# Delta rule and feed-forward on one core: the first stretch of the feed-forward written out in joint bursts

## Chip, core and metric

The kernel runs on one core of a Trainium2 chip. A core has five engines with a queue each: TensorE (PE, matmuls and transposes, with its weight loads shown apart), VectorE (DVE), ScalarE (ACT), GpSimd (POOL) and SyncE (SP), which here issues nearly all transfers. Each engine works its own instructions in the order of the program and waits where an operand isn't ready. The metric is the device time of one execution in microseconds (us). Before the change it is 678.54 us, the median of 4 runs (677.17 to 681.86).

## What is computed

A delta-rule attention over 4 sequences of 768 tokens with 8 heads of 48 dimensions, and behind it a feed-forward block with a PReLU, 384 to 2048 to 384, all in float32:

```python
k_n = k / (np.linalg.norm(k, axis=-1, keepdims=True) + 1e-06)
for t in range(S):
    kt, vt, bt = (k_n[:, :, t], v[:, :, t], beta[:, :, t, None])
    y[:, :, t] = np.einsum('bhd,bhde->bhe', q[:, :, t], state)
    v_old = np.einsum('bhde,bhd->bhe', state, kt)
    state = state + bt[:, :, :, None] * np.einsum('bhd,bhe->bhde', kt, vt - v_old)
x = y.transpose(0, 2, 1, 3).reshape(B * S, H * D)
h = x @ w_in
g = np.maximum(h, 0.0) + alpha * np.minimum(h, 0.0)
return g @ w_out
```

## The kernel before, in words

**Chunks and steps.** The 768 tokens are cut into 12 chunks of 64. Within a chunk the recurrence is written as a triangular system, so that it becomes matmuls. A step is one chunk of one pair of sequences; there are 24, and steps 2c and 2c + 1 make chunk c. Steps 0 and 1 are done ahead of everything in `first_chunk`. The stretch that the change touches holds steps 2 and 3, together with the feed-forward's first layer for chunk 0.

**What a step needs.** `flips` transposes keys and queries (128x128 transposes, line 360) and ACT copies them out (381, 383). `squares` and `weigh` make the norms and weights: ACT 330, 340, 341, DVE 332, 347, POOL 349, 350. `grams` multiplies keys with keys (407) and DVE weights the result into `same` and `right` (413); POOL copies a part on (456). Four steps together are turned (`turn_in`, DVE 472) and eliminated on DVE. For the first four steps only 16x16 blocks are eliminated; `cross` puts the 32x32 inverses together from them with 32x32 products: 576, an ACT copy (581), 586 and 593, then DVE adds (600, 602). `placing` lays the inverses into `diag` and `inv` (ACT 631) and copies weights (652). `between_1` (663) and `between_2` (677) make the 64x64 inverse, with an ACT copy (669) and a DVE addition (684) behind them. `through_state` multiplies with the state (713, 718) and DVE subtracts and masks (728, 427), ACT copies `y` (736). `solve` is 743 with DVE 747, `outputs` 756 with 762, `next_state` 772 with 780. `to_ffn` transposes `y` (795) into `xt` (ACT 797).

**The feed-forward's first layer.** `ffn_in(0)` issues 48 products of 128 rows by 256 columns (884), in eight groups of six. Each group has one of two PSUM banks; ACT 894 and DVE 896 empty it. `IN_PARTS` is 48.

**The weights.** `w_in` and `w_out` come from memory as float32 words that are converted in pieces. A piece is a pair of ACT instructions (208, 209) and a pair of DVE instructions (218, 223), and a fetch by SP (192) where a staging place comes free. `conv_in` and `conv_out` are the generators of these; the touched stretch has 22 halves of pieces.

**What sets the order.** The queues are written by hand: every engine executes what the program emits, in that order. `weave` takes several generators and a number of parts for each, and draws from them in turn in proportion. `part(g, n)` draws n parts; `chain` puts generators behind each other.

**Around the change.** Before it, `first_chunk` ends with the transposes of steps 0 and 1. In the stretch itself one `weave` draws from four sources: the products of `ffn_in(0)`; the attention of steps 2 and 3 (`in_turn(*later)`, `ready(2)`, `pair(2)`); the weight pieces; and `statics(4, 7)`, the transposes and Grams of steps 4 to 7. Within `cross` a callback (`aside`) puts one product of `ffn_in(0)` between every four or eight blocks. Behind the stretch comes a `weave` of the remaining `w_out` pieces, `ffn_in(1)`, more `statics`, and the elimination of steps 4 to 7.

Small tiles in PSUM come from `ps_big`, which has three buffers of two banks in rotation: a new one has to wait until the one three allocations earlier has been emptied.

## Time and profile before

| what | before |
|---|---|
| median of 4 runs | 678.54 us |
| profiled execution | 680.26 us |
| its span | 678.5 us |
| PE busy | 657.1 us (97%) |
| DVE busy | 453.3 us (67%) |
| ACT busy | 263.7 us (39%) |
| POOL busy | 35.5 us (5%) |
| PE busy, 50.5 to 97.0 us | 45.58 of 46.50 us |
| DVE busy, same stretch | 31.88 us |
| ACT busy, same stretch | 29.77 us |
| mean busy share of the DMA engines, same stretch | 0.73 |
| granted TensorE clock, same stretch | 1.00 |

The busy time of PE is a time in which a matmul was under way, and not a measure of how well it was used: matmuls are pipelined, and a row's duration contains its way through the array. What a matmul costs the stream is therefore read from the starts of consecutive rows. The idle time in brackets on a timeline's row is what the engine waited before it, with the instruction that released it.

### The profile page before, as it was taken

The numbers are of one execution on the slowest core, as the hardware profiler recorded it, in microseconds if no ns is written. First come the engines' busy times: TensorE is split into PE (matmuls) and PEld (weight loads), VectorE is DVE, ScalarE is ACT, GpSimd is POOL, SyncE is SP. The second block draws the span as 40 slices with busy tenths as digits, with TensorE's granted clock in tenths as the row PEclk, the third lists the DMA queues.
The fourth block names the chain that finished last, engine by engine and source line by source line (L and its number), as shares of the span: only waits on it lengthen the run. The fifth ranks groups of instructions, "written<-read, shape, count | busy, mean of one in ns | idle before, by whom it ended". The sixth has DMA issues, their size and how long they took to land.

```text
span 678.5 us, 21573 instructions
## 1 busy us (share of the span) xinstructions
PE 657.1 (97%) x9359; PEld 572.6 (84%) x9359; DVE 453.3 (67%) x1125; ACT 263.7 (39%) x624; POOL 35.5 (5%) x105
## 2 busy tenths in 40 slices
PE   5999998999998999999999999999999999999997
PEld 4577777656687998988998988988989989989997
DVE  4955788878989868758858758859655355354251
ACT  5926756335455343344353342243234134021110
POOL 6000211101000000001000000000000000000000
PEclk9979999999999999999999999999999999999999
DMA  8937854211332022122111112111121110100000
GB/s 123 242 90 203 201 116 117 71 30 30 71 76 49 12 62 48 25 48 49 26 37 37 26 37 37 26 40 33 26 46 27 36 37 2 33 5 2 23 1 25
DMA packets 110960, 37.69 MB, mean 56 GB/s; under 512 B 104161, under 2 KB 107249, under 8 KB 110865
## 3 DMA queue, kind: packets, MB, share of 16 engines
q1 hardware_dynamic: 109088, 35.81, 24.2%
q8 instruction: 74, 1.21, 0.7%
q10 hardware_dynamic: 1776, 0.49, 0.4%
q14 instruction: 22, 0.17, 0.1%
HBM read 31.56 MB, written 4.72 MB: 53 GB/s over the span
## 4 chain that ended last, share of the span: by engine, by line
PE 81%; DVE 11%; ACT 4%; SPq 2%; issue 1%; DMA 0%; POOL 0%; DVEq 0%
PE p_ffn L884 33%; PE p_ffn L948 27%; PE p_big L360 2%; PE p_big L713 2%; PE p_big L743 2%; PE p_big L756 2%; PE p_big L663 2%; DVE prod L499 2%; PE p_big L677 2%; DVE block L505 2%; PE p_big L1104 2%; SPq L120 1%; PE p_big L718 1%; PE p_big L407 1%; PE p_big L772 1%
## 5 line engine op out<-in xcount | busy, mean ns | idle before, releaser
L884 PE MATMUL p_ffn<-xt,w_in 128*128 128x256 f32 x1152 | 265.2, 383 | 5.1 <-DVE act L896 2.3
L884 PEld LDWEIGHTS p_ffn<-xt,w_in 128*128 128x128 f32 x1152 | 213.3, 190 | 35.1 <-ACT sums L894 2.2
L896 DVE SCALAR_TENSOR_TENSOR act<-act,al_t,p_ffn 128x256 f32<-128x256 f32 x176 | 76.5, 476 | 82.1 <-ACT act L894 82.1
L894 ACT ACTIVATE act<-p_ffn 128x512 f32<-128x512 f32 x88 | 52.4, 596 | 146.6 <-PE p_ffn L884 146.2
L948 PE MATMUL p_ffn<-w_out,act 128*128 128x192 f32 x480 | 82.5, 328 | 0.1
L948 PEld LDWEIGHTS p_ffn<-w_out,act 128*128 128x128 f32 x480 | 77.6, 190 | 1.1 <-issue 0.5
L505 DVE TENSOR_TENSOR block<-block,prod 128x30 f32<-128x30 f32 (+9 forms) x150 | 49.9, 333 | 5.1
L499 DVE TENSOR_TENSOR prod<-block 128x30 f32<-128x30 f32 (+9 forms) x150 | 48.8, 325 | 3.3 <-POOL block L489 1.6
L968 DVE TENSOR_TENSOR o_sb<-u,p_ffn 128x192 f32<-128x192 f32 x40 | 13.4, 353 | 52.2 <-PE p_ffn L948 41.9
L797 ACT COPY xt<-p_big 128x384 f32<-128x384 f32 x22 | 10.4, 477 | 75.7 <-PE p_big L795 75.7
L736 ACT COPY y<-p_big 128x384 f32<-128x384 f32 x22 | 10.5, 477 | 51.4 <-PE p_big L718 49.9
L948 PE MATMUL p_ffn<-space_out,sums 128*128 128x192 f32 x160 | 29.4, 327 | 0.0
L948 PE MATMUL p_ffn<-more,sums 128*128 128x192 f32 x160 | 29.3, 326 | 0.0
L948 PE MATMUL p_ffn<-w_out,sums 128*128 128x192 f32 x160 | 27.6, 326 | 0.0
L948 PEld LDWEIGHTS p_ffn<-more,sums 128*128 128x128 f32 x160 | 26.5, 190 | 0.0
L948 PEld LDWEIGHTS p_ffn<-space_out,sums 128*128 128x128 f32 x160 | 26.5, 190 | 0.1
L948 PEld LDWEIGHTS p_ffn<-w_out,sums 128*128 128x128 f32 x160 | 26.3, 190 | 0.0
L689 ACT COPY inv<-p_big 32x256 f32<-32x256 f32 x38 | 13.8, 362 | 29.4 <-DVE u L747 29.2
L631 ACT ACTIVATE diag<-inverse,which 64x128 f32<-64x128 f32 (+2 forms) x60 | 24.2, 405 | 2.1 <-DVE inverse L472 1.3
L728 DVE TENSOR_TENSOR r<-v_raw,p_big 64x192 f32<-64x192 f32 (+1 forms) x66 | 23.2, 352 | 1.0
L349 POOL TENSOR_TENSOR beta_t<-beta_t,rec 128x8 f32<-128x8 f32 x24 | 6.6, 274 | 304.3 <-DVE rec L347 283.7
L713 PE MATMUL p_big<-beside,k_t 48*64 48x112 f32 x704 | 21.4, 259 | 0.6 <-DVE right L413 0.6
(156 smaller groups left out, 950.7 us busy)
## 6 DMA issues: line engine op xcount, KB each, us to landing
w_out<-in_moe_w_in_dram SPq DMA_DIRECT2D x12, 512.0 KB, 4.9
qp<-in_q_dram SPq DMA_DIRECT2D x48, 96.0 KB, 3.0
v_raw<-in_v_dram SPq DMA_DIRECT2D x48, 96.0 KB, 2.9
kl<-in_k_dram SPq DMA_DIRECT2D x96, 48.0 KB, 2.6
out_dram<-o_sb SPq DMA_DIRECT2D x92, 48.0 KB, 1.6
space_out<-in_moe_w_out_dram SPq DMA_DIRECT2D x11, 384.0 KB, 3.7
ke<-in_k_dram SPq DMA_DIRECT2D x43, 96.0 KB, 3.3
w_out<-in_moe_w_out_dram SPq DMA_DIRECT2D x5, 384.0 KB, 4.0
```

What stands on the lines that cost most here:

```text
L360: nc.tensor.transpose(p[0:ROWS, g * 128 : (g + 1) * 128], src[:, 2 * g : 2 * g + 2].rearrange("p h d -> p (h d)")[:, 0:ROWS], ident,)
L499: nc.vector.tensor_tensor(out=prod, in0=r[:, 0:j, j : j + 1].to_broadcast([128, j, n]), in1=r[:, j : j + 1, j + 1 : HB].to_broadcast([128, ...
L505: nc.vector.tensor_tensor(out=r[:, 0:j, j + 1 : HB], in0=r[:, 0:j, j + 1 : HB], in1=prod, op=ALU.add)
L631: nc.scalar.mul(out, x, which[rows, i : i + 1])
L663: nc.tensor.matmul(p[half(t ^ a if changes(n) else t), a, g], right[n % EARLY][half(t), a * G + g : a * G + g + 2].rearrange("p b i -> p ( ...
L689: nc.scalar.copy(to[rows], p[rows])
L713: nc.tensor.matmul(p[half(t ^ a), a, g], k_t[n][dims(a), g, half(t)], beside[bp][dims(a), t, g])
L728: nc.vector.tensor_tensor(out=r[to, a], in0=v_in[to, a], in1=p[own, a, :, 0:D], op=ALU.subtract)
L884: nc.tensor.matmul(p_h[:, i], w_in[:, t, (f + i) * 128 : (f + i + 1) * 128], xt[:, t], start=(t == 0), stop=(t == KT - 1),)
L894: nc.scalar.activation(g, p_h, ACT.Relu, scale=-1.0)
L896: nc.vector.scalar_tensor_tensor(out=g[:, i], in0=g[:, i], scalar=al_t[:, f + i : f + i + 1], in1=p_h[:, i], op0=ALU.mult, op1=ALU.add,)
L948: nc.tensor.matmul(p, x(i), w(i), start=(i == 0), stop=(i == FP - 1))
```

## The change

The `weave` of the stretch is replaced by a function that writes the order out. At its head the 32x32 products of steps 2 and 3 come in three bursts: the 576 of both steps, then 586 and 593 of step 2, then those of step 3. Behind them are five joint bursts, in which steps 2 and 3 do the same operation one after the other, three of them followed by the Gram of one of the steps 4 to 6; the Gram of step 7 comes last. Between the bursts stand 4 to 6 products of `ffn_in(0)`, with 1 to 3 weight pieces and, once, the six placements woven into them by `alongside`. The transposes of steps 4 to 7 follow directly on a burst. `through_state` and `solve` of both steps now share one PSUM buffer for their small results, and `outputs` and `next_state` of a step share one. The functions `pair`, `ready` and `in_turn` and two constants go. The loads are issued from within the new function.

```diff
-    PAIR = 6
-    def pair(n):
...
-    READY = 5
-    def ready(n):
...
-    def in_turn(*gens):
...
-    n = PARTS_IN - n + 10
+    assert n + 22 == PARTS_IN + 10
 
     first_in = ffn_in(0)
-    later = [
-        cross(0, slice(x * H, x * H + H), edge, half_way, lambda: next(first_in, None))
-        for x in (2, 3)
-    ]
-    weave(
-        (first_in, IN_PARTS - 10), (chain(in_turn(*later), ready(2), pair(2)), 2 * CROSS + READY + PAIR),
-        (chain(conv_in, part(conv_out, 10)), n), (statics(NJ, 2 * NJ - 1), 2 * NJ + 1),
-    )
+    convert_on = chain(conv_in, part(conv_out, 10))
+
+    def alongside(products, pieces, *gens):
+        weave((part(first_in, products), products), (part(convert_on, pieces), pieces), *gens)
+
+    def second_pair():
+
+        n = 2
+        both, x = (n, n + 1), NJ
+        halves = [cross(0, slice(i * H, i * H + H), edge, half_way) for i in both]
+        squares(x)
+        alongside(4, 2)
+        for h in halves:
+            next(h)
+        flips(x, n)
+        load_early(x + NKE)
+        load_q(n + 2)
+        squares(x + 1)
+        alongside(5, 2)
+        next(halves[0])
+        flips(x + 1, n + 1)
+        load_early(x + 1 + NKE)
+        load_q(n + 3)
+        now(weigh(x))
+        place(n, (0,))
+        alongside(4, 2)
+        next(halves[1])
+        now(weigh(x + 1))
+        place(n + 1, (0,))
+        alongside(4, 2)
+        for i in both:
+            now(between_1(i))
+        now(grams(x))
+        squares(x + 2)
+        alongside(5, 3, (chain(*(placing(i, (1, 2, 3)) for i in both)), 6))
+        for i in both:
+            now(between_2(i))
+        now(grams(x + 1))
+        for i in both:
+            scale_v(i)
+        flips(x + 2, N)
+        load_early(x + 2 + NKE)
+        now(weigh(x + 2))
+        alongside(5, 3)
+        y = ps_big()
+        pieces = []
+        for i in range(2):
+            pieces += through_state(n + i, None, y[:, :, i * G * D : (i + 1) * G * D])
+        now(pieces)
+        squares(x + 3)
+        alongside(5, 3)
+        y = ps_big()
+        pieces = []
+        for i in range(2):
+            pieces += solve(n + i, y[:, :, i * G * D : (i + 1) * G * D])
+        now(pieces)
+        now(grams(x + 2))
+        flips(x + 3, N)
+        load_early(x + 3 + NKE)
+        now(weigh(x + 3))
+        alongside(5, 2)
+        pieces = []
+        for i in both:
+            y = ps_big()
+            pieces += outputs(i, y[:, :, 0 : G * D]) + next_state(i, y[:, :, G * D : 2 * G * D])
+        now(pieces)
+        for i in both:
+            load_late(i + 2)
+            load_v(i + 3)
+        alongside(5, 2)
+        for i in both:
+            to_ffn(i)
+        now(grams(x + 3))
+        alongside(IN_PARTS - 42, 1)
+
+    second_pair()
     fetch_out(len(stages))
```

## The prediction

> **What bounds the kernel now.** I read the page first. It says 678.5 us of span, 680.26 for the profiled execution with what lies around it, and TensorE (PE) carries 81% of the chain that ended last. So a microsecond of PE time in the touched stretch is a microsecond of the kernel, unless PE is waiting there anyway.

> ```profile
> span 678.5 us, 21573 instructions
> ...
> PE   5999998999998999999999999999999999999997
> ...
> PE 81%; DVE 11%; ACT 4%; SPq 2%; issue 1%; DMA 0%; POOL 0%; DVEq 0%
> ```

> Next the timeline of PE from the first product of chunk 0 (50.55) to its last (about 96.75): 46.2 us. A product is two passes of 256 columns, shown as x2; columns are start, duration, engine, line, instruction, count, and in brackets idle time and releaser.

> ```profile
> 51.18 0.44 PE L576 MATMUL p_big<-turned,sums 32*32 32x16 f32 x32
> 51.55 0.70 PE L884 MATMUL p_ffn<-xt,w_in 128*128 128x256 f32 x2
> 52.18 0.44 PE L576 MATMUL p_big<-turned,sums 32*32 32x16 f32 x32
> ...
> 59.02 0.64 PE L593 MATMUL p_big<-inverse,act 32*32 32x16 f32 x32
> ...
> 74.35 1.12 PE L677 MATMUL p_big<-diag,mid 64*64 64x32 f32 x32 [0.23 <-ACT diag L631]
> ...
> 81.92 1.00 PE L713 MATMUL p_big<-beside,k_t 48*64 48x112 f32 x32 [0.64 <-DVE right L413]
> ...
> 105.21 2.83 PE L884 MATMUL p_ffn<-xt,w_in 128*128 128x256 f32 x12 [1.84 <-ACT sums L894]
> ...
> 112.92 4.15 PE L884 MATMUL p_ffn<-xt,w_in 128*128 128x256 f32 x18
> 117.00 0.69 PE L407 MATMUL p_big<-k_t 48*64 48x64 f32 x32
> ```

> See the alternation: PE swaps between full-width products and small tiles 21 times in these 46 us. Starts give the price: a run of 18 passes between tiles takes 117.00 - 112.92 = 4.08, a run of 2 takes 52.18 - 51.55 = 0.63. The slope is 3.45 / 16 = 0.216 a pass, and 0.20 is left per run, paid at its two edges. The row 87.46 to 88.52 (4 passes, 1.06) lies on the same line. Against transposes (full width too) an edge costs nothing: 54.48 - 53.52 = 0.96 for 4 passes with one such edge.

> Last, the chain just behind the stretch, from VectorE's (DVE) timeline:

> ```profile
> 94.80 0.42 DVE L413 TENSOR_TENSOR same<-p_big,wgt 128x256 f32<-128x256 f32 x1
> ...
> 96.48 2.33 DVE L472 STREAM_TRANSPOSE block<-same 128x256 f32<-128x256 f32 x4 [0.93 <-POOL same L456]
> 98.70 0.32 DVE L218 TENSOR_SCALAR w_out<-w_out 128x384 uint32<-128x384 uint32 x1
> ```

> Here PE isn't the bound. Gram 7 (407, ends 94.25) is weighted by DVE (413), copied by POOL (456), turned (472); then come 896, 332, 340, 347, 349, 489 and 499 in queue order, and only then 896 frees the bank on which PE waits until 105.21. What counts is therefore when gram 7's chain starts, not only when the products end.

> **The change, part by part.**

> *Fewer runs.* In the compiled order of the changed kernel the 21 tile bursts become 9: 576 in one; 586 with 593 twice; 663 with a Gram; 677 with a Gram; 713/718 of both steps; 743 with a Gram; 756/772 of both; the last Gram. No matmul is added or dropped. Products now: 25.0 us (starts to next starts). After: 48 x 0.43 = 20.6, plus 10 runs x 0.20, less four edges that lie on transposes (0.4): 22.2. **Gain 2.8.** [...] The row gives 24 x 0.10 = 2.4, near my 2.8. [...]

> *The tiles themselves* gain nothing from being joined: 576 x128 passes took 1.53 in one run in the first chunk (28.48 to 30.01), 4 x 0.37 = 1.48 here. All of them stay at 20.2 us, transposes included.

> *Stalls removed.* 0.64 before 713 (behind DVE's 413: that Gram now has five products between), 0.23 before 677, and 0.19 in the 593 that took 0.56 where others take 0.37. **Gain 1.06.**

> *Stall added: 677.* ScalarE (ACT) must place the second halves of `diag` (631). I add the queue from its own rows, by intervals between starts. PE reaches 663 at 50.55 + 13.8 = 64.35 and ends it at 66.2. ACT places `diag` of step 3 (it waits on DVE's 600) at 64.75: 0.45; 208/209: 0.72 + 0.58, so 66.5; two 669: 0.6; 330: 0.42; 894: 0.49; 208/209: 1.30; then 631: 0.50, done 69.8. PE has a Gram (0.6) and five products (2.35) as cover and is there at 69.15: waits 0.65. Step 3's `diag` now stands behind `inv` of step 2 and two 652 (0.45 + 0.42), done 71.1, when the first 677 half ends at 70.85: 0.25 more. **Loss 0.9.** Behind it in ACT's queue only step 3's `inv` and 381 wait, both with slack. Bounds: 0 if ACT runs a microsecond ahead, 2.5 if the last `w_in` piece is late: it stands in that queue and lands at 62.37 + 5.3 = 67.7, ACT reaches it at 68.0, so 0.3 of slack; late by 2 it costs 1.7 more. SP issues it where it did, paced by earlier landings.

> *The other joints*, by the same addition. 586 needs the 581 copies (done 54.2, PE there at 57.0). 663 needs `diag` of step 3: 65.25 against 65.25, slack nil, 0 to 0.5, I take 0. 743 needs `r` of step 3: done 79.75, PE 80.9. 756 needs `u`: 83.9 against 85.6. Transposes of `y`: 88.4 against 90. Each has a microsecond or more. [...] Behind 713/718 the rows give DVE 2 x (1.08 + 0.69) = 3.5 us. The cover is half the burst (1.4, step 2's share starts there) plus five products 2.35: 3.75, so no stall; if emptying began only after the burst, 1.15 would be bare. The two 736 copies wait for both 718 now, 1.4 later for step 2; their reader is the transpose, ten microseconds on.

> *SP and POOL.* Loads of k 7, 8, 9 and of q 4, 5 are issued in another order (k 8 between the q loads); they wait on transposes that are no later, and SP stands behind its landings until 65 anyway. `w_out`'s four fetches stay behind k 9: 74.9 instead of 76.2; read by ACT from 81.6, landing takes 4.0: hidden. POOL's 349/350 of step 7 go behind two 456: hidden, their reader is the last Gram. `fetch_out` is unmoved. The helpers taken out issue nothing else.

> *The chain behind.* At the last product: 2.8 + 1.06 - 0.9 = 3.0. Behind gram 7 lies 2.7 us of PE, not 2.5, so it is 3.2 earlier. 413 waited 0.55 behind 780; now it stands behind 896 of the seventh pair, which ends 0.13 after the Gram: 0.4 more. One 218 (0.3) moves ahead of 472. Sum: **3.9 earlier** at the wait that ends at 105.21; PE would be there at about 99.4, so DVE's chain decides. Behind it PE is full until 150 (its waits there are local), so 3.9 stays: 680.26 - 3.9 = 676.4 for the profiled kind of execution, **674.6** on the median of the runs shown (678.54).

> **Rivals.**
> 1. *Gain half eaten*: `w_in` lands late or 663 and 677 are both fed late, 2.4 instead of 0.9: 3.9 - 1.5 = 2.4, time 676.1. For it: slacks of 0.3 and nil. Against: DVE is busy 31.9 of 46.5 us, ACT 29.8; neither is full.
> [...]
> 3. *Slower: in-order queues at the joints.* Before each of five joints (663, 677, 743, 756, transposes) a weight conversion stands in ACT (1.15 to 1.30) and DVE (1.1). If these bodies, not the products, time the burst, each of the five is bare by about 1.5: 7.5 instead of 0.9, 3.9 - 6.6 = -2.7, 681.2. It decides from 0.95 per joint (4.8 in all). For it: the chain of waits runs through ACT and DVE from 72.0 to 81.9 already. Against: computed slack over a microsecond at three of the five.
> 4. *The chain behind doesn't move*: then only the wait grows, 678.5. Against: its links all follow gram 7 in queue order; none is timed by a transfer. That the regrouping doesn't happen is excluded by the compiled order.

> **How the numbers follow.** Forecast 0.50 (own range 673.5 to 675.8), rival 1 0.16, rival 2 0.12, rival 3 0.17, rival 4 0.05. A measurement here tells about 0.5%, 3.4 us, from no change: the bound is at 675.1. Faster: three quarters of the forecast, all of rival 2, a little of rival 1: 0.55. Slower (over 681.9): the worse half of rival 3 and its tail: 0.16. Same: 0.29. The range runs from 672.6 (rival 2 with no stall at 677) to 680.3 (the milder part of rival 3); about 2 in 10 stay out.

> **What would show it.** Right: product runs of 8 to 12 passes still 0.216 each plus 0.2; nine bursts; a wait before 677 of 0.5 to 1.5 put down to ACT's 631; gram 7 ending near 91; the third run of chunk 1's products starting near 101.3 behind a wait under 2. Wrong: waits over 0.5 before 743, 756 or the transposes (rival 3); ACT's 208 waiting for a DMA near 68 (rival 1); 105 unmoved (rival 4). It fails altogether if joined bursts run slower inside than their rows.

## The result, and the profile after

| | before | after |
|---|---|---|
| median of the runs | 678.98 us (63 runs) | 676.94 us (44 runs) |
| ratio, 95% interval | | 0.9968, 0.9955 to 0.9981 |
| profiled execution / span | 680.26 / 678.5 us | 684.86 / 683.0 us |
| T0: first product of chunk 0 starts | 50.55 | 53.00 |
| R: third run of chunk 1's products starts, behind its wait | 105.21 | 109.78 |
| X = R - T0 | 54.66 | 56.78 |
| span - R | 573.3 | 573.2 |

The change gains 2.2 us by this ratio (1.3 to 3.1), where 3.9 were forecast. The profiled execution of the changed kernel is a disturbed one, 8 us above its median. That makes it useless for the size of the gain, and very useful for what disturbs the kernel. The page, with the row of PE, the instruction queue and the chain:

```profile
span 683.0 us, 21580 instructions
...
PE   5988898999999999999999999999999999999997
...
q8 instruction: 74, 1.21, 0.7%
...
PE 81%; DVE 10%; ACT 3%; issue 2%; DMA 1%; SPq 1%; POOL 0%; ACTq 0%; DVEq 0%; POOLq 0%
```

PE still carries 81% of the chain. "Issue", time in which the engine waited for nothing that the profile shows, has gone from 1% to 2%. The timeline of PE shows where, in the rows that answer to those of before:

```profile
53.00 1.99 PE L884 MATMUL p_ffn<-xt,w_in 128*128 128x256 f32 x8 [0.62 <-ACT xt L797]
54.92 0.78 PE L576 MATMUL p_big<-turned,sums 32*32 32x16 f32 x70
55.88 0.67 PE L576 MATMUL p_big<-turned,sums 32*32 32x16 f32 x58 [0.17 <-issue]
...
60.17 0.34 PE L593 MATMUL p_big<-inverse,act 32*32 32x16 f32 x18
63.00 0.83 PE L593 MATMUL p_big<-inverse,act 32*32 32x16 f32 x44 [2.49 <-issue]
63.76 1.10 PE L360 MATMUL p_big<-ident,ke 128*112 128x128 f32 x4
...
72.85 0.60 PE L407 MATMUL p_big<-k_t 48*64 48x64 f32 x23
74.73 0.34 PE L407 MATMUL p_big<-k_t 48*64 48x64 f32 x7 [1.28 <-issue]
75.00 2.43 PE L884 MATMUL p_ffn<-xt,w_in 128*128 128x256 f32 x10
78.08 1.12 PE L677 MATMUL p_big<-diag,mid 64*64 64x32 f32 x32 [0.65 <-ACT diag L631]
79.42 1.06 PE L677 MATMUL p_big<-diag,mid 64*64 64x32 f32 x29 [0.22 <-ACT diag L631]
...
83.70 1.00 PE L713 MATMUL p_big<-beside,k_t 48*64 48x112 f32 x32
...
94.98 0.92 PE L884 MATMUL p_ffn<-xt,w_in 128*128 128x256 f32 x3
96.48 1.78 PE L884 MATMUL p_ffn<-xt,w_in 128*128 128x256 f32 x7 [0.58 <-issue]
...
109.78 2.83 PE L884 MATMUL p_ffn<-xt,w_in 128*128 128x256 f32 x12 [1.83 <-ACT sums L894]
```

Three readings.

First, the bursts and the known waits are as the forecast put them. The 0.64 before 713 is gone, ACT's 631 is waited for before 677 (0.65 and 0.22), and 1.83 is left before the third run.

Second, waits on "issue" stand inside the bursts, in the middle of one and the same operation, where the profile shows no operand missing: 0.17, 2.49, 1.28, 0.58. Count the passes between the first two: 58 of 576, 8 transposes, 10 of 884, 32 of 586 and 20 of 593 are 128. A pass is two instructions, weight load and matmul (9359 of each on the page), and now and then a semaphore instruction of PE stands between passes. Counted with these, the trace has 256, 512 and 1024 instructions from one of the four waits to the next, and 18,927 in the whole kernel, which is 73.9 times 256. The instruction queue, q8, moved 74 packets of 1.21 MB / 74 = 16 KB.

The trace's records of q8 give each packet's time. The packets behind the four waits landed at 54.35, 61.52, 73.27 and 95.13, and PE went on 1.53, 1.48, 1.46 and 1.35 us later. The same holds for every wait on "issue" of 0.15 us or more between 15 and 180 us, in all 16 traces: 51 waits, each ending 1.25 to 1.9 us behind the landing of a packet of q8. **PE waits there for its own program**, which comes in blocks of 256 instructions, 128 passes or a few less. That is the theory tested below; I call it A.

Third, behind the 2.49 the four transposes take 1.10, and four in other places 0.60 to 0.65. The windows of the same kernel (stretch, then busy time of PE, PEld, DVE, ACT and POOL, then granted clock, DMA share, GB/s):

```profile
58.00:60.00 2.00, 2.00 (x30) 1.51 (x31) 0.88 (x2) 1.97 (x5) 0.00 (x0) 1.00 1.02 203
60.00:62.00 2.00, 0.51 (x42) 0.41 (x36) 1.13 (x4) 0.84 (x2) 0.00 (x0) 1.00 0.52 83
62.00:64.00 2.00, 1.00 (x45) 0.96 (x46) 0.47 (x2) 0.00 (x0) 0.00 (x0) 0.69 0.33 58
64.00:66.00 2.00, 2.00 (x10) 1.91 (x10) 0.73 (x3) 0.25 (x1) 0.00 (x0) 0.50 0.63 111
```

The granted clock was 0.50 there (half clock, from here on). By narrower windows the half lasted from 62.8 to 66.2, and it cost 1.4 us: the eight transposes took 1.75 us from start to start (63.76 to 65.51), and 0.93 at their first place (56.47 to 57.40); the rest of 593 and the eight products behind lost 0.6 against the same rows of the next profile.

The account of the two profiled executions closes: T0 is 2.45 later, in code that the change doesn't touch; X is 2.12 longer; the rest is equal. Together 4.57, and the spans differ by 4.5. The comparisons below use X, therefore, and the ratio over many runs.

### The profile page after: what moved, and what is told of

Its sections match the earlier page's. It is cut to its first block, busy times and chain, and to the rows that moved or that the text cites. A ratio compares the mean times of both kernels' runs of the same rounds, so it can differ in the third digit from the quotient of the medians.

```text
span 683.0 us, 21580 instructions
## 1 busy us (share of the span) xinstructions
PE 656.4 (96%) x9359; PEld 574.4 (84%) x9359; DVE 453.7 (66%) x1125; ACT 263.3 (39%) x624; POOL 35.7 (5%) x105
## 3 DMA queue, kind: packets, MB, share of 16 engines
q8 instruction: 74, 1.21, 0.7%
## 4 chain that ended last, share of the span: by engine, by line
PE 81%; DVE 10%; ACT 3%; issue 2%; DMA 1%; SPq 1%; POOL 0%; ACTq 0%; DVEq 0%; POOLq 0%
PE p_ffn L884 33%; PE p_ffn L948 27%; PE p_big L360 3%; PE p_big L713 2%; PE p_big L743 2%; PE p_big L756 2%; PE p_big L663 2%; DVE prod L499 2%; PE p_big L1102 2%; PE p_big L677 2%; DVE block L505 2%; PE p_big L718 1%; PE p_big L772 1%; PE p_big L407 1%; DMA ke<-in_k_dram 1%
## 5 line engine op out<-in xcount | busy, mean ns | idle before, releaser
L884 PE MATMUL p_ffn<-xt,w_in 128*128 128x256 f32 x1152 | 261.2, 382 | 5.2 <-ACT sums L894 1.8
L884 PEld LDWEIGHTS p_ffn<-xt,w_in 128*128 128x128 f32 x1152 | 215.0, 190 | 35.5 <-ACT sums L894 2.2
L894 ACT ACTIVATE act<-p_ffn 128x512 f32<-128x512 f32 x88 | 52.3, 594 | 144.5 <-PE p_ffn L884 144.1
L631 ACT ACTIVATE diag<-inverse,which 64x128 f32<-64x128 f32 (+2 forms) x60 | 24.3, 405 | 2.1 <-DVE inverse L472 1.3
L689 ACT COPY inv<-p_big 32x256 f32<-32x256 f32 x38 | 13.8, 362 | 29.4 <-DVE u L747 29.2
L332 DVE TENSOR_REDUCE norm<-ksq 128x8 f32<-128x384 f32 x24 | 13.0, 544 | 12.8 <-ACT ksq L330 12.8
```

The costliest lines, as they stand in the source:

```text
L631: nc.scalar.mul(out, x, which[rows, i : i + 1])
L689: nc.scalar.copy(to[rows], p[rows])
L884: nc.tensor.matmul(p_h[:, i], w_in[:, t, (f + i) * 128 : (f + i + 1) * 128], xt[:, t], start=(t == 0), stop=(t == KT - 1),)
L894: nc.scalar.activation(g, p_h, ACT.Relu, scale=-1.0)
```

## The experiments

Theory A: PE has to wait for a block of instructions where 128 passes take less time than the delivery of the next block; the joined bursts make such places, and the forecast priced bursts without it. Theory B: the edges between tiles and products were mispriced. Theory C: the joints starve (the forecast's rival 3). In the tables, "ratio" is against the kernel before on the same chip.

**The changed kernel again** (no edit).

> The changed kernel once more, for a second profile, since the first one comes from an execution of 684.86 us against a median of 676.94. Theory A (PE's instructions arrive in blocks of 256, one block at a time; where matmuls are small and the DMA engines are full, PE runs dry): the time is near 677, the wait before 677 is again 0.9 us from ACT, the waits named 'issue' stand again after pass 70 of the 576 burst, near pass 20 of the first 593, near pass 25 of the Gram behind 663, but sum to 1.5 to 2.5 us instead of 4.5. Theory B (the edges between full-width and tile runs are cheaper than 0.20 us): no 'issue' wait over 0.3, product runs of 10 passes take 2.25 instead of 2.36. Theory C (queues of ACT and DVE at the joints): waits over 0.5 on ACT or DVE before 743, 756 or 795.

Measured: 677.79 us, ratio 0.9962 (0.994 to 0.9984). Its profile has T0 at 54.54 and X = 51.62, that is 3.0 less than before. PE's timeline:

```profile
56.46 1.44 PE L576 MATMUL p_big<-turned,sums 32*32 32x16 f32 x128
...
58.76 2.32 PE L884 MATMUL p_ffn<-xt,w_in 128*128 128x256 f32 x10
...
62.06 0.56 PE L593 MATMUL p_big<-inverse,act 32*32 32x16 f32 x44 [0.19 <-issue]
...
69.83 1.06 PE L663 MATMUL p_big<-diag,right 64*64 64x32 f32 x29 [0.33 <-ACT diag L631]
...
82.69 2.42 PE L884 MATMUL p_ffn<-xt,w_in 128*128 128x256 f32 x10
85.05 1.15 PE L743 MATMUL p_big<-r,inv 64*64 64x48 f32 x64
...
92.84 1.78 PE L884 MATMUL p_ffn<-xt,w_in 128*128 128x256 f32 x7 [0.57 <-issue]
...
95.21 0.69 PE L407 MATMUL p_big<-k_t 48*64 48x64 f32 x32
95.83 3.29 PE L884 MATMUL p_ffn<-xt,w_in 128*128 128x256 f32 x14
...
106.16 2.83 PE L884 MATMUL p_ffn<-xt,w_in 128*128 128x256 f32 x12 [1.84 <-ACT sums L894]
```

The same kernel, the same places (20 passes into 593; 3 into the 884 behind 756/772), but 0.19 where the other execution waited 2.49, none at 407, and the clock stayed at 1.00 through the stretch. The waits on "issue" sum to 0.76, less than the 1.5 to 2.5 that theory A expected. This is a stretch with little disturbance (ahead of T0 the execution had half clock for 20.5 us). It answers theory B as well. A run of 10 passes between two tile bursts takes 85.05 - 82.69 = 2.36, which is 10 x 0.216 and two edges of 0.10. The run from 58.76 takes 61.01 - 58.76 = 2.25; it has a transpose on one side, so one edge less. Edges cost what they were priced at. And no wait stands before 743, 756 or 795: theory C has nothing to show.

Why did the same border cost 0.19 here and 2.49 there? The packet itself took 1.26 us here, 1.32 there. It began 2.2 us after PE had passed the border before it here (at about 57.2; the packet at 59.38), and 4.3 us after it there (55.88 and 60.20). In e6, below, it was 3.1 us, and the wait 0.90. So the late start of the packet makes the wait. What held it back isn't shown.

**The kernel before again.**

> The kernel before once more, for a second profile of it. Theory A (instruction blocks): from the first product of chunk 0 to the third run of chunk 1's products it takes 54.7 us again (between 54 and 57), with at most 0.5 us of waits named 'issue' in the stretch, since its small matmuls are thinned by products; from that third run to the end of the span 573.2 us, as in the four profiles of the changed order so far. If the kernel before has such waits of 1 us and more too, the blocks don't explain the shortfall.

Measured: 678.81 us, X = 54.44, no "issue" in the stretch, and 0.28 and 1.02 in `first_chunk`, which is tile bursts. The stretch of before was steady (54.66 and 54.44). That of after is not (51.62 and 56.78).

**Move the borders of the blocks.** The opening burst of `busy` is half a unit or a unit shorter, and tiny matmuls stand in its place. All blocks behind then begin some 30, 62 or 94 passes earlier in the program; the stretch itself is unchanged. Here half a block:

```diff
-    busy(BUSY)
+    p = ps_one()
+    busy(7, p)
+    for x in range(32):
+        i = quad(x % 4)
+        nc.tensor.matmul(p[i, 0:LB], ident[i, 0:HB], ident[i, 0:LB])
```

(A quarter: `busy(7.5, p)` and 16 of them. Three quarters: `busy(7, p)` and 48. An expectation below calls the opening burst of the quarter longer; it is shorter by half a unit.)

> The changed kernel with one of the eight filling matmuls before the first chunk replaced by 32 tiny ones (128 instructions of PE, a filling of about the same length), so that every later border of 256 instructions lies 64 passes earlier in the work. Theory A: the 'issue' waits move with it, to pass 6 of 576, into the products or the 586 behind them, and away from the Gram behind 663; the time moves by 0.5 us or more either way. Theories B and C: nothing moves, time within 0.5 us of the changed kernel.

Measured: 684.17 us, ratio 1.0062 (1.004 to 1.0083), X = 55.04. The waits of PE moved with the borders:

```profile
38.14 0.61 PE L593 MATMUL p_big<-inverse,act 32*32 32x16 f32 x28 [2.26 <-issue]
...
61.68 4.11 PE L884 MATMUL p_ffn<-xt,w_in 128*128 128x256 f32 x10 [1.18 <-issue]
```

The first row is of `first_chunk`. In the second, the wait that stood 20 passes into 593 now stands before the first 884 of the next run, which is 62 passes earlier in the program: the amount of the shift. Nothing that a theory of operands knows about was moved. Behind it the clock halved (62.1 to 65.5), and this run of 10 passes took 4.1 us instead of 2.3. The other two positions agree: in e8 the wait stands 29 passes earlier than in the unshifted kernel, at pass 23 of 586 (0.38 us), and in e9, where the border falls 34 passes later, at pass 54 of 593 (0.86 us). Theory A's place is shown.

The same shift on the kernel before, then the other two positions on both kernels:

> The kernel before with the same 128 instructions put in as e2 had. The first chunk is the same code in both, so its part of e2's loss must come here too. Theory A: the wait of about 2.3 us in the first chunk's 593 (near pass 100) comes here as in e2, and the stretch, whose small matmuls are thinned by products, loses less than in e2: from 54.5 to 55 or 56 us, time 680.5 to 683, that is 1 to 3 us below e2. If e2's loss lies in the joint bursts alone: 679. If the change gains nothing but a lucky position of the borders: this one is as slow as e2, 684, or slower.

> The changed kernel with 16 tiny matmuls put into the filling ahead of the first chunk, so that every later border of 256 instructions lies 32 passes earlier. Theory A: 'issue' waits stand 32 passes earlier than in the changed kernel (pass 38 of the 576 burst, the end of the first 586, the start of the Gram behind 663), not where e2 had them; the time lies between 675 and 684 and differs from the changed kernel by more than 0.5. If the loss in e2 came from the shorter filling: no slower than the changed kernel, and no moved waits.

> The kernel before with the shift of e8_shift_quarter (the opening burst half a unit longer and 16 tiny matmuls, so the borders of the instruction blocks move by about 30 passes). e8 gave 1.0032 for the changed kernel at this position. If the change gains its forecast 3.9 us at every position and borders cost both kernels alike: before must come out at 1.0090 (686.5 us or so less the rest, 685 to 686). If the gain belongs to the position of the borders alone: 1.003, no different from e8. Theory A takes no side between these for one position; it expects 1.003 to 1.009, with waits of PE on nothing that the profile shows, 128 passes apart, in the dense places of both.

> The changed kernel with every later border of 256 instructions 94 passes earlier (48 tiny matmuls for one filling matmul). Theory A: 'issue' waits at passes that lie 94 before those of the changed kernel (or 34 behind): near pass 104 of the 576 burst, in the second half of the first 593, near pass 14 to 20 of the 677 burst; a time that differs from the changed kernel by more than 0.5 us, most likely slower as with the two other shifts (678 to 684).

> The kernel before with the shift of e9_shift_three_quarters (48 tiny matmuls at the head). e9 gave 1.0047 for the changed kernel here. Gain at every position: before at 1.010. Gain of one position alone: 1.0047. Theory A expects something between, and over the four positions (as written, quarter, half, three quarters) a mean gain below the forecast 0.57%.

| shift, passes | before: ratio | after: ratio | difference | before: X | after: X |
|---|---|---|---|---|---|
| none | 1 | 0.9968 | -0.0032 | 54.66, 54.44 | 56.78, 51.62 |
| about 30 | 1.0033 (1.0014 to 1.0053) | 1.0032 (1.0008 to 1.0057) | -0.0001 | 54.51 | 54.51 |
| about 62 | 1.0058 (1.0029 to 1.0087) | 1.0062 (1.004 to 1.0083) | +0.0004 | 55.04 | 55.04 |
| about 94 | 1.0083 (1.0053 to 1.0113) | 1.0047 (1.0024 to 1.007) | -0.0036 | 54.48 | 52.15 |

Read it by columns. The shift costs both kernels something, and most of what the profiles show of it in the kernel before is ahead of T0, in `first_chunk`, which is the same dense code in both (waits there of 2.26 in e2, 1.80 in e8, 1.36 in e10). The mean clock of the runs of before falls too, from 0.995 to 0.991, 0.989 and 0.985. The shift also shortens the opening burst, and no run separates that from the borders.

In the stretch, X of the kernel before hardly moves, 54.4 to 55.0, though in e10 it has a wait on "issue" of 0.61. X of the changed kernel moves from 51.6 to 55.0, and the ratios go along with it: where X is 2.3 to 3.0 shorter, the kernel gains 0.32 to 0.36%; where X is equal, nothing is gained.

That is agreement and not proof. Each X is of one execution, and without a shift two executions of the changed kernel gave 56.78 and 51.62. In e2 and e8 X contains a half clock of 3.4 us. And at the two positions without gain the changed kernel's runs had the lower mean clock, 0.9891 against 0.9911 at the quarter and 0.9849 against 0.9890 at the half; whether that comes from the change, or was met by chance ahead of T0, isn't shown. In e8 the stretch held these two waits, besides shorter ones at 586 and 663, and the clock halved from 72.2 to 75.6:

```profile
88.41 0.45 PE L407 MATMUL p_big<-k_t 48*64 48x64 f32 x13 [0.68 <-issue]
94.55 0.67 PE L772 MATMUL p_big<-u,kl 64*64 64x48 f32 x29 [1.31 <-issue]
```

The expectation that before would lose less than after from the half shift fell, and so did both simple answers set for the other two positions: by these ratios the gain belongs neither to all positions nor to one. The mean of the four differences is -0.0016, about 1.1 us. The intervals are some 0.2 to 0.3% wide on either side, so the two zeros are "nothing that can be seen".

**The price of a block by itself.** 256 tiny matmuls (512 passes) in one burst at the start of the next phase, where the DMA engines have little to do. It adds work and changes no result.

```diff
+    p = ps_one()
+    for x in range(256):
+        i = quad(x % 4)
+        nc.tensor.matmul(p[i, 0:LB], ident[i, 0:HB], ident[i, 0:LB])
     late = ffn_out(1)
```

> The price by itself: 256 independent 32x32 matmuls (512 passes, 1024 instructions) put in at about 147 us, where the DMA engines are nearly idle. At the rate of the 576 burst (12 ns a pass) they take 6.1 us. Theory A: after the first one or two borders PE waits at every border of 256 instructions, the gaps are named 'issue', and a block of 128 passes takes 3 to 4.5 us (a transfer of 1 us and what lies around it): 10 to 16 us in all. If instructions come fast enough when the DMA engines are idle: 6 to 7 us without gaps.

Measured: 692.65 us. The instruction queue and PE's timeline:

```profile
q8 instruction: 78, 1.28, 0.8%
...
142.86 1.86 PE L1376 MATMUL p_big<-ident 32*32 32x16 f32 x201
147.44 1.90 PE L1376 MATMUL p_big<-ident 32*32 32x16 f32 x128 [2.72 <-issue]
151.44 1.90 PE L1376 MATMUL p_big<-ident 32*32 32x16 f32 x128 [2.10 <-issue]
155.17 0.94 PE L1376 MATMUL p_big<-ident 32*32 32x16 f32 x55 [1.83 <-issue]
```

The 1024 added instructions came in 4 packets more, 78 instead of 74, and exactly 128 passes lie between waits. They take 1.9 us (at half clock, from 147.2) and come every 4.00 and 3.73. The records of q8 show what such a period is made of: the next packet starts 1.1 to 1.2 us after PE has begun a block (147.44 and 148.63, 151.44 and 152.54, 155.17 and 156.29), the packets take 1.3 to 1.5 us, and PE goes on 1.3 to 1.5 us after a packet has landed. The first 201 passes run without a wait: the 73 that were left of one block, and the block behind it. So one block lay ready ahead. That is what this burst shows: **128 passes, done in 1.9 us, are followed by a wait until 3.7 to 4.0 us have passed**, once what was in store has been used.

**The same burst with full DMA engines.** Six loads of 512 KB into a tile that is free there are issued from ACT's queue ahead of the burst.

```diff
+    for x in (3, 0, 1, 2, 3, 0):
+        nc.scalar.dma_start(
+            out=spare[:, x * 1024 : x * 1024 + 1024],
+            in_=moe_w_in[x % 3 * 128 : x % 3 * 128 + 128, 0:W_IN_P].bitcast(U32),
+        )
```

> The dense burst of 256 tiny matmuls (512 passes) as in e4_dense, with six loads of 512 KB (rows of w_in, into a tile that is free there and written again later) issued from ScalarE's queue just ahead of it. It adds 512 passes; the output is not touched. Theory A with contention (an instruction block travels through the same DMA engines as the loads): the waits inside the burst that stood 128 passes apart grow from about 2.1 us to 4 to 6 us while the DMA engines are full, a block then takes 5 to 7 us instead of 3.7 to 4.0, and the burst some 18 to 22 us instead of 13. Rival (the price of a block is the sequencer's own and the load in the DMA engines is a coincidence): the blocks stay at 3.7 to 4.0 us, the burst at 13 us, the kernel near 692.5.

Measured: 701.87 us.

```profile
148.54 1.86 PE L1382 MATMUL p_big<-ident 32*32 32x16 f32 x201
154.75 1.90 PE L1382 MATMUL p_big<-ident 32*32 32x16 f32 x128 [4.35 <-issue]
158.48 1.90 PE L1382 MATMUL p_big<-ident 32*32 32x16 f32 x128 [1.83 <-issue]
164.40 0.94 PE L1382 MATMUL p_big<-ident 32*32 32x16 f32 x55 [4.02 <-issue]
```

The first and the last wait grew, from 2.72 to 4.35 and from 1.83 to 4.02; the middle one did not. The windows within the three waits (clock, DMA share and GB/s are the last three columns):

```profile
152.00:153.00 1.00, 0.00 (x0) 0.00 (x0) 0.00 (x0) 0.00 (x0) 0.00 (x0) 0.92 1.00 381
157.00:158.00 1.00, 0.00 (x0) 0.00 (x0) 0.00 (x0) 0.00 (x0) 0.00 (x0) 0.50 0.60 157
161.00:162.00 1.00, 0.00 (x0) 0.00 (x0) 0.00 (x0) 0.00 (x0) 0.00 (x0) 0.50 0.82 307
```

By the records of q8 the packets took no longer here: 0.93 to 0.96 us, against 1.3 to 1.5 in e4. They started later: the first 3.9 us into the burst instead of 1.7, the last 3.6 us after its block had begun (158.48 and 162.13) instead of 1.1. With loads beside it, then, the start of a packet came up to 2.5 us later: that the load is only a coincidence falls. But it needn't, the middle packet started after 1.5 us, its block came at the rate of e4 with a share of 0.6 to 0.95 beside it, and the burst took 165.28 - 148.54 = 16.7 us, less than the 18 to 22 expected. Each of the two bursts is one execution. In the changed kernel's head the share is 0.72 to 1.02 from 54 to 60 us, and there a block took 63.00 - 55.88 = 7.1 us in one execution and about 4.9 in the other (from the 70th pass of 576, at about 57.2 by its rate, to 62.06).

**Undo the head alone.** The 32x32 products get their products of `ffn_in(0)` back as company (the `aside` of before), the rest of the change stays.

```diff
-        halves = [cross(0, slice(i * H, i * H + H), edge, half_way) for i in both]
+        halves = [
+            cross(0, slice(i * H, i * H + H), edge, half_way, lambda: next(first_in, None))
+            for i in both
+        ]
-        alongside(4, 2)
+        alongside(2, 2)
```

(The other three counts of the head: 5, 4, 4 become 3, 1, 1.)

> The changed kernel with the products put back between the pieces of the 32x32 work, as the kernel before had them; the joint bursts stay. Seven tile bursts more than the changed kernel. Theory A: 1.4 us of edges lost, part of it given back by fewer 'issue' waits in the head: 676.5 to 677.5, and no 'issue' wait over 1 us in the first 12 us of the stretch. Theory B (cheap edges): the same time as the changed kernel within 0.5 and no other waits. My forecast as it stood: 1.4 slower than the changed kernel.

Measured: 680.34 us, ratio 1.0007 (0.9982 to 1.0031), X = 57.11. From T0 to 663 it takes 15.44 us instead of 13.84 in e1: the edges put back cost 1.6 (1.8 with e1's wait of 0.19 taken off), near the 1.4 that the forecast's prices give. No "issue" is left in the head. But it is not saved either, it comes in the bursts behind:

```profile
67.91 0.49 PE L407 MATMUL p_big<-k_t 48*64 48x64 f32 x7 [1.43 <-issue]
...
92.37 1.78 PE L884 MATMUL p_ffn<-xt,w_in 128*128 128x256 f32 x7 [2.04 <-issue]
```

**Three tries to keep the gain.** Move the loads of k, v and `w_out` behind the head, to leave the DMA engines to the instructions there:

```diff
-            load_late(i + 2)
-            load_v(i + 3)
...
-    fetch_out(SPACES)
...
         place(n + 1, (0,))
+        load_v(n + 1)
+        fetch_out(SPACES)
+        load_late(n)
+        load_late(n + 1)
+        load_v(n + 2)
         alongside(4, 2)
```

> The changed kernel with four groups of loads (late keys of steps 2 and 3, values of steps 3 and 4) and three fetches of output weights issued behind the second 32x32 burst, instead of ahead of the stretch. Theory A: the DMA engines are freer while the head takes its blocks of instructions, so the 'issue' wait in the first 593 goes to 0 and the time is 0.5 to 1.5 below the changed kernel, unless the fetches now collide with the Gram behind 663. If the loads are late for their readers: waits on DMA before 756 or 208. If the DMA engines have no part in it: the same 'issue' waits and the same time within 0.5.

Measured: 678.27, ratio 0.9991 (0.9967 to 1.0015), X = 52.21, "issue" 0.90 in 593. The share from 50 to 58 us stayed at 0.79 to 1.01, because the last fetch for `w_in` (66.26 in e1) and the next loads of keys and queries (from 69.32 in e1) moved up into the room. It says nothing about contention, then, since the load wasn't lowered; it is no gain.

Give 677 more cover (two products more ahead of it, one less in each of two later runs):

```diff
-        alongside(5, 3, (chain(*(placing(i, (1, 2, 3)) for i in both)), 6))
+        alongside(7, 3, (chain(*(placing(i, (1, 2, 3)) for i in both)), 6))
```

> The changed kernel with seven products instead of five between 663 and 677, taken from the two joints ahead of 756 and of the transposes of y. The wait of 0.9 before 677 should be gone and no other should come: 0.9 below the changed kernel, 676.0 to 677.0 by the same measure. If ScalarE is late because of PE and not the other way round (the placements wait for PE), the wait stays.

Measured: 679.01, ratio 0.9991 (0.9961 to 1.0021), X = 52.90. The wait for `diag` is gone, and 0.93 stands behind it at the transposes (360), for DVE's 684; "issue" of 1.45 and 0.18 is where it was in kind. The stall had only been passed on.

Thin the last burst (two products and a piece between step 2's and step 3's part of 756/772):

```diff
+            if i == n:
+                alongside(2, 1)
         now(pieces)
...
-        alongside(5, 2)
+        alongside(3, 1)
```

> The changed kernel with two of the five products that follow the outputs put between the outputs of step 2 and those of step 3. In four profiles of the changed order PE waited 0.57 to 0.63 us ('issue') at the third pass of those five products, one block of 128 passes behind the start of the outputs. Theory A: two products stretch that block by 1.06 us, so that wait goes to 0 or below 0.2, and one more run costs 0.20: 0.4 less from the first product to the third run of chunk 1 in the profile; by time not told from the changed kernel. If the wait has another cause it stays at 0.6.

Measured: 677.52, ratio 0.9975 (0.9953 to 0.9998), X = 52.27. The wait at this border is 0.82 instead of 0.57, where theory A's expectation had none or below 0.2. The border moved by just the four passes put in: in e1 it came 3 passes into the products (92.84), here it comes before the last pass of 772 (93.05), so the block has 4 passes of products in it instead of 3 and is hardly longer. The packet also started later, 1.8 us after the first 756 instead of 1.3 (90.73 and 88.94; 90.62 and 89.35 in e1). None of the three beats the change as it was written.

## Why the prediction was wrong

The saving of edges was priced rightly, and the sign was right. The size, -3.9 against -2.2, was not. By its own steps, with the profile of e1 (ends are the starts of the next rows):

| step | forecast | measured |
|---|---|---|
| gram 7 ends earlier, from T0 | 3.0 + 0.2 | 43.70 - 41.29 = 2.41 |
| chain behind gram 7 shorter | 0.4 + 0.3 | 10.96 - 10.33 = 0.63 |
| X shorter | 3.9 | 3.04 |
| stall at 677 | -0.9 | -(0.65 + 0.22) = -0.87 |
| stall at 663 | 0 | -0.33 |
| waits for instructions in the stretch | none priced | -0.76 here, -4.52 in the other profile, and 1.4 for its half clock |

- *Fewer runs, stalls removed*: right. The 21 bursts are nine, runs of 10 take 0.216 a pass and 0.10 an edge, and the wait before 713 is gone. Without the 0.76 and the 0.33, X would be 4.1 shorter; the terms sum to 3.9. That these are so near is partly luck: the products took 2.55 us less instead of 2.8 (24.96 and 22.41, starts to next starts), and the tiles, put at nothing, took 0.9 less up to gram 7 (17.04 and 16.03, of which 0.15 was a wait).
- *The 0.19 inside 593*: counted among the stalls that the change removes, it was the very thing that the forecast left out. PE stood there from 59.20 to 59.35, 1.4 us behind a packet of q8 that landed at 57.97. In e5 it isn't there (57.88 to 58.25, 0.37).
- *677*: right to 0.03, by adding up ACT's queue from its rows. *663*: slack "nil, 0 to 0.5, I take 0" was 0.33, as ACT waits for DVE's 600 there. An end computed at zero slack should have been priced at the middle of its bounds.
- *The other joints, `w_in`, the chain*: right. No wait before 743, 756 or 795, ACT waits for no transfer in the stretch, the third run waits 1.84.
- *"Behind it PE is full ... so 3.9 stays"*: right, span - R is 573.2 to 573.3 in both, and in every run that has nothing added behind.
- **The step that failed**: *"The tiles themselves gain nothing from being joined ... All of them stay at 20.2 us"*. That priced bursts at the rate of their rows, with the delivery of their instructions at nothing and without a reason. In the stretch of before, the products between the tiles stretched every 128 passes: some 46 us for about a thousand passes is 5.8 us a block, above the 3.7 to 4.0 us in which a block came in e4, and PE waited 0.15 us in one profile and not at all in the other. The change takes the products out of the bursts. Now the 128 passes of 576 are done in 1.4 us, the block from there into 593 needs 4.7 (57.2 to 62.06, less 0.19), and others are slower than before. The mean is nearly the same, but no more than one block lay ready ahead in e4 (201 passes ran before the first wait), so the dense places wait: 0.76 us in e1, 4.52 in the first profile. The prediction's own condition for total failure was "if joined bursts run slower inside than their rows"; they don't run slower, they stop in the middle, in some executions for 2.5 us.

It could have been seen. The profile of before has waits on "issue" in `first_chunk`, where tiles stand undiluted (0.62 at a 663), and "issue 1%" in the chain, which I showed and didn't follow. Where the products prevail, the borders cost nothing that shows: behind 100 us PE has no wait on "issue" in the four profiles of the two unshifted kernels. For tiles, e4 shows 1.8 to 2.7 us bare at each border.

The low end of the range, 672.6, and the 0.12 of rival 2 suppose edges dearer than 0.10 us. No run shows one: the run of 10 passes in e1 took 2.36 us, 10 x 0.216 and two edges of 0.10.

How much of the missing 1.7 us is which stays open in part. X of e1 shows 0.9 of it (3.9 - 3.0). The clocks of the runs show a little more. A mean clock of 0.999 or 1.000 leaves no room for a half clock of 3.4 us. At such a clock the changed kernel's median is 675.7 (15 runs) and that of before 678.2 (75 of the 166 runs of it made beside the experiments; 677.9 to 678.6 from chip to chip). So the gain is about 2.5 there, and 1.4 of the missing 1.7 has nothing to do with half clock. A mean clock of 0.997 is one half clock of 3.4 us (0.5 x 3.4 of 678). Of the changed kernel's 66 runs, e1's included, 20 have it, at a median 1.0 us above those at full clock; of before, 5 of the 166 (0.996 or 0.997). So the change does bring a half clock into some executions, and over all runs it costs about 0.3 us (an estimate, 20/66 of 1.0). The remaining 0.5 stays open; waits like the first profile's, at full clock, are a candidate that no profile shows. Open too is what starts a packet late in one execution and not in the next; that DMA load can do it is shown in e12, that it did so in the stretch is not.

## What to carry to other kernels

Gathering small matmuls into bursts saves the edges between tile shapes, 0.10 us each here, but the program has to be delivered too: where 128 passes (256 instructions of PE) were done in 1.9 us, PE stopped at the block's border until 3.7 to 4.0 us were up (e4), and up to 5.9 with loads beside it (e12). So aim at blocks of 128 passes that each last longer than their delivery; no run here gained by it yet (e3 paid as much in edges, and e11 did not lengthen its block). Count the passes from one "issue" wait to the next to find the borders, and test a change of a few us at more than one position of them before believing its gain.
